# First MLP product in three float32r products of 12-bit parts, in place of a seven-product float32 scheme

## The chip, the cores and the metric

The kernel runs on one core of a Trainium2 chip, in one launch. The metric is the device time of the program in microseconds, as the median of several runs. Three runs of the kernel before gave 356.90, 357.06 and 355.76 us: a median of 356.9.

## What is computed

The first part is a state-space layer (Mamba2) over 4 batches, 8 heads, 768 tokens, head dimension 32 and state dimension 16. The second is a two-layer MLP with a hard-swish between its products. Cut to what matters:

```
for each chunk of tokens:                  # x, a, B, C are inputs; float32
    cum   = cumsum(log(clip(a)))
    M     = (C B^T) * exp(cum_i - cum_j), causal
    y     = M x + (C state) * exp(cum_i)
    state = exp(cum_end) * state + sum_j exp(cum_end - cum_j) B_j x_j
X = y reordered to (3072 tokens, 256)
h = X @ w_in                               # 256 x 2048
g = h * clip(h + 3, 0, 6) / 6
out = g @ w_out                            # 2048 x 256
```

The weights arrive as 8-byte floats (their raw words are read) and are decoded to float32 on the chip.

## The kernel before, in words

**Blocks.** The 768 tokens are cut into 6 blocks of 128. Block `k` of all four batches is 512 columns of MLP work. The outer loop `for k in range(NC)` (L993) runs the MLP of block `k` and, woven in between, the attention part of block `c = k + 1` and loads and decays of block `ahead = k + 2`. The order of every engine's queue is the order in which the program text issues the instructions (the pools run under a manual schedule), and each engine works its queue in that order. SP issues nearly all DMAs, in the same way.

**Decoding of weights.** `decode(i)` (L187) turns one of eight pieces of 8-byte words into float32: pieces 0 to 3 are `w_in` (512 of the 2048 columns each, both halves of the contraction), pieces 4 to 7 are `w_out`. Each piece is five steps: an ACT copy (L198), three VectorE operations on integers (L215, L217, L201), two ACT activations (L221, L223) with a VectorE operation (L205), and two VectorE operations that finish (L228, L236). Pieces 0 and 1 are made before block 0's product, the others are woven into it.

**Block 0.** `mlp_in` (L613) makes a column tile `f` of `h` (128 of the 2048 hidden columns by 512 tokens) with two float32 matmuls of 128x512. ACT's `ramp` (L694) takes Relu(h/6 + 1/2) into `gT` and VectorE's `times_ramp` (L699) caps it at 1 and multiplies it by `h`. Four PSUM banks (f0 to f3) rotate. Then `first_out` (L703) makes the output with plain products, and VectorE makes sums of weights (`weight_sums`, L729; `in_weight_sums`, L632). The attention of block 1 is placed between its parts; `results(c)` runs `mix` (the last attention matmuls), `keep` (four ACT copies of y from PSUM to `yT`, L608) and `sum_y` (four VectorE sums of y halves, L655). Two tiles later `lead(c, 0)` begins the product of block 1.

**Blocks 1 to 5, first product.** Hidden columns are taken in pairs of tiles (`s` of 8), and a 2x2 block scheme with seven products of 128x256 in place of eight computes both (`lead`, `early`, `middle`, `last`; every matmul is L658). It uses sums of `w_in` made once and sums of `yT` made per block. In each pair, ACT copies a partial product to a second bank (L673) and one to SBUF (L680), VectorE copies one (L674) and adds two (L686, L687); then come two `ramp` and two `times_ramp`.

**Blocks 1 to 5, second product.** `wide_units` (L827, matmuls L836; the last block `out_units`, L760, matmuls L772) makes the output with a seven-product scheme, in 14 steps of 8 float32 matmuls; the loop over these steps carries `scores`, `multiply`, `decay_ends`, `results` of the next block. At step 12 the next block's `lead` is issued. GpSimd makes the sums of `gT` for it (`g_sums`, L758), the masks (`conceal`, L158) and some small products (L396, L403).

Of the kernel before, what the change touches and what calls it, by code (L numbers as in the profile page):

```python
# [8 lines left out]
FP32 = mybir.dt.float32  # L9
U32 = mybir.dt.uint32  # L10
# [10 lines left out]
def kernel(  # L21
# [34 lines left out]
    NQ = NH // 2  # L56
    HU = NH // 2
# [57 lines left out]
    def load_x(c):  # L115
        sl = slice(c * P, (c + 1) * P)
        xts[c] = loads.tile([P, NB * NH, D], FP32, name="xt")
        nc.sync.dma_start(out=xts[c], in_=x[:, :, sl, :].rearrange("b h s d -> s (b h) d"))

    w_in = const.tile([P, NK, DF], FP32, name="w_in")  # L120
    w_sum = const.tile([P, NF // 2, P], FP32, name="w_sum")
# [50 lines left out]
    nc.vector.memset(half, 0.5)  # L172
    bias_hi = const.tile([P, 1], FP32, name="bias_hi")
# [12 lines left out]

    def decode(i):  # L187
# [7 lines left out]
        s = att.tile([P, n], U16, name="ws")  # L195
        e = att.tile([P, n], U16, name="we")
# [33 lines left out]
        if i < NP:  # L230
            dst = w_in[:, :, i * FP * P:(i + 1) * FP * P]
            m, e = (t.rearrange("p (k f) -> p k f", k=NK) for t in (m, e))
        else:
            dst = w_out[:, (i - NP) * FP:(i - NP + 1) * FP, :]
            m, e = (t.rearrange("p (k f) -> p k f", k=FP) for t in (m, e))
# [8 lines left out]
    picks = const.tile([P, G * N], BF16, name="picks")  # L244
# [77 lines left out]

    yTs, states, mids, bTs, bss, tmps = {}, {}, {}, {}, {}, {}
# [67 lines left out]
    def ends(c, b):  # L391

        if b == 0:
            bss[c] = att.tile([P, G, N], FP32, name="bs")
        hs = slice(b * NH, b * NH + NH)
        nc.gpsimd.tensor_tensor(  # L396
            out=bss[c][:, hs], in0=Bs[c][:, hs],
            in1=Ls[c][:, b, :, HT - 1:HT].to_broadcast([P, NH, N]), op=ALU.mult)
# [174 lines left out]
    def renew(c):  # L573

        states[c] = att.tile([P, NB, 2 * D], FP32, name="state")
        later = att.tile([P, NB, 2 * D], FP32, name="later", bufs=1)
        nc.vector.tensor_tensor(
            out=later, in0=mids[c], in1=etos[c][:, :, P - 1:P].to_broadcast([P, NB, 2 * D]),
            op=ALU.mult)
        new_state(states[c], adds[c], later)  # L580
# [22 lines left out]
    def keep(c):  # L603

        yTs[c] = att.tile([P, NK, NB, P], FP32, name="yT")
        for a, u in ((0, 0), (0, 1), (1, 0), (1, 1)) if c else ((0, 0), (1, 0), (0, 1), (1, 1)):
            y, dst = ys[c][a, u], yTs[c][:, u, :, HALF[a]]
            nc.scalar.copy(out=dst, in_=y)  # L608
# [4 lines left out]
    def mlp_in(k, f):  # L613
        h = ps.tile([P, NK, 2 * P], FP32, name="h", tag=f"f{f % 4}")
        for j in range(NK):
            nc.tensor.matmul(  # L616
                out=h.rearrange("p r i -> p (r i)"), lhsT=w_in[:, j, f * P:(f + 1) * P],
                rhs=yTs[k][:, j].rearrange("p b i -> p (b i)"),
# [10 lines left out]
    wi = w_in.rearrange("p k (j e c) -> p k e j c", e=2, c=P)  # L629
    in_sums, y_sums, evens, odds, parts_of = {}, {}, {}, {}, {}  # L630

    def in_weight_sums():  # L632
        for h in range(2):
            js = slice(h * NJ // 2, (h + 1) * NJ // 2)
            a11, a12, a21, a22 = (wi[:, k, e, js] for e in range(2) for k in range(2))
            s1, s2 = (att.tile([P, NJ // 2, P], FP32, name="w_sum", tag=t) for t in ("ws", "we"))
            s4 = w_sum[:, js]
            for o, p_, q_, op in ((s1, a21, a22, ALU.add), (s2, s1, a11, ALU.subtract),
                                  (s4, a12, s2, ALU.subtract), (a21, a11, a21, ALU.subtract)):
                nc.vector.tensor_tensor(out=o, in0=p_, in1=q_, op=op)  # L640
            for n, t in ((1, s1), (2, s2), (3, a21), (4, s4)):
                in_sums.setdefault(n, []).extend(t[:, i] for i in range(NJ // 2))
            yield

    def y_half(k, j, r):
        return yTs[k][:, j, 2 * r:2 * r + 2].rearrange("p b i -> p (b i)")

    def sum_y(k):
        ts = att.tile([P, 3, 2 * P], FP32, name="ts", bufs=1)
        t1, t2, t4 = (ts[:, i] for i in range(3))  # L650
        t3 = y_half(k, 0, 1)
        y_sums[k] = {1: t1, 2: t2, 3: t3, 4: t4}
        for o, p_, q_ in ((t1, t3, y_half(k, 0, 0)), (t3, y_half(k, 1, 1), t3),
                          (t2, y_half(k, 1, 1), t1), (t4, y_half(k, 1, 0), t2)):
            nc.vector.tensor_tensor(out=o, in0=p_, in1=q_, op=ALU.subtract)  # L655

    def half_product(bank, r, lhsT, rhs, start=False):
        nc.tensor.matmul(  # L658
            out=bank[:, r], lhsT=lhsT, rhs=rhs, start=start, stop=True, skip_group_check=True)

    def lead(k, s):

        (pool, tag), (pool_e, tag_e) = (
            ((ps, "f0"), (ps, "f2")), ((ps, "f1"), (ps, "f3")),
            ((ps_y, "y0"), (ps_y, "y1")))[s % 3]
        odds[k, s] = odd = pool.tile([P, 2, 2 * P], FP32, name="odd", tag=tag)
        evens[k, s] = even = pool_e.tile([P, 2, 2 * P], FP32, name="even", tag=tag_e)
        parts_of[k, s] = up = ffn.tile([P, 2, 2 * P], FP32, name="up", bufs=2)  # L670
        half_product(odd, 1, wi[:, 0, 0, s], y_half(k, 0, 0), start=True)
        half_product(odd, 0, in_sums[3][s], y_sums[k][3])
        nc.scalar.copy(out=even, in_=odd[:, 1:2].to_broadcast([P, 2, 2 * P]))  # L673
        nc.vector.tensor_copy(out=up[:, 1], in_=odd[:, 0])  # L674

    def early(k, s):
        even = evens[k, s]
        half_product(even, 0, wi[:, 1, 0, s], y_half(k, 1, 0))
        half_product(even, 1, in_sums[2][s], y_sums[k][2])
        nc.scalar.copy(out=parts_of[k, s][:, 0], in_=even[:, 1])  # L680

    def middle(k, s):
        even, odd, up = evens[k, s], odds[k, s], parts_of[k, s]
        half_product(odd, 0, wi[:, 1, 1, s], y_sums[k][4])
        half_product(even, 1, in_sums[1][s], y_sums[k][1])
        nc.vector.tensor_tensor(out=odd[:, 0], in0=odd[:, 0], in1=up[:, 0], op=ALU.add)  # L686
        nc.vector.tensor_tensor(out=odd[:, 1], in0=even[:, 1], in1=up[:, 1], op=ALU.add)  # L687

    def last(k, s):
        half_product(evens[k, s], 1, in_sums[4][s], y_half(k, 1, 1))  # L690
# [12 lines left out]
    def first_out(b, i, c):  # L703
# [6 lines left out]
        for f in range(i * FP, (i + 1) * FP):  # L710
            if b == NB - 1 and f == NF - 2:
                lead(c, 0)
            nc.tensor.matmul(  # L713
                out=o[:, b % 2], lhsT=gTs[0][:, f, b * P:(b + 1) * P], rhs=w_out[:, f],
                start=(f == 0 and b % 2 == 0), stop=True, skip_group_check=True)
        if i == NP - 1 and b % 2:
            ob = ffn.tile([P, 2, DM], FP32, name="ob", bufs=2)
# [11 lines left out]
    def weight_sums():  # L729


        t3 = const.tile([P, NJ, P], FP32, name="t3")
# [27 lines left out]
    def out_units(k):  # L760
# [15 lines left out]
        for t in range(2):  # L776
# [9 lines left out]
            if t == 0:  # L786
                unit(oa, 0, quarter(0, 0, 0), w4[:, 0, 0], rest)
                unit(oa, 3, quarter(0, 0, 1), w4[:, 0, 0], rest)
                x1 = ffn.tile([P, 2, P], FP32, name="x1")
# [6 lines left out]
            res = ffn.tile([P, 5, P], FP32, name="res", bufs=2)  # L796
# [7 lines left out]
            u = ffn.tile([P, 2, P], FP32, name="u", bufs=2)  # L804
# [108 lines left out]
    def results(c, parts=range(2)):  # L913
        mix(c, parts)
        keep(c)
        sum_y(c)
# [4 lines left out]

    def load(c):
        load_bc(c)
        load_x(c)
# [60 lines left out]
    load(1)  # L985


    weave = {}
# [4 lines left out]
    for k in range(NC):  # L993
        gTs[k] = ffn.tile([P, NF, TB], FP32, name="gT")
        c, ahead = k + 1, k + 2
        if k == 0:
            for f in range(NF):
                mlp_in(k, f)
                for i in weave.get(f, []):
                    weights(i, 1)  # L1000
                if f in (6, 8):
                    diff_exp(c, f // 2 - 3)
            load(ahead)
# [3 lines left out]
            sums, sums_in = weight_sums(), in_weight_sums()  # L1007
            for i in range(NP):
                for b in range(NB):
                    first_out(b, i, c)  # L1010
                    if (i, b) == (0, 0):
                        weights(NP + 3, 1)
                        weights(NP + 2, 1)
                        weights(NP + 3, 3)
                        rows(ahead)
                    elif (i, b) == (1, 0):
                        next(sums_in)
                        next(sums_in)
# [16 lines left out]
                    elif (i, b) == (3, 1):  # L1035
                        results(c)
                        next(sums)
                        decay_ends(ahead, 3)
                    elif (i, b) == (3, 3):
# [3 lines left out]
        for s in range(NJ):  # L1043
            early(k, s)
            if s == 0:
                if ahead < NC:
                    load(ahead)
                if c < NC:
                    carry(c)
            if s < NJ - 1:  # L1050
                lead(k, s + 1)
            if s:
                last(k, s - 1)
                ramp(k, 2 * s - 2, evens[k, s - 1])
            middle(k, s)
            if s:
                times_ramp(k, 2 * s - 2, evens[k, s - 1])
            ramp(k, 2 * s + 1, odds[k, s])
            times_ramp(k, 2 * s + 1, odds[k, s])
            if s in (1, 3) and ahead < NC:  # L1060
                conceal(ahead, s // 2)
            if s in (3, 5) and c < TURN:
                turn(c, s // 4)
            if s in (2, 4, 6):
                g_sums(k, s - 2)
        for i, _ in enumerate((wide_units if c < NC else out_units)(k)):
            if i == 0:
                s = NJ - 1
                last(k, s)
                ramp(k, 2 * s, evens[k, s])  # L1070
                times_ramp(k, 2 * s, evens[k, s])
                g_sums(k, s - 1)
                if k == 1:
                    next(sums)
            if c < NC:
# [11 lines left out]
                if i == (7 if c == TURN else 6):  # L1087
                    results(c, (1,) if c == TURN else range(2))
                    if ahead < NC:
                        from_start(ahead)  # L1090
# [4 lines left out]
                if i == 12:  # L1095
                    lead(c, 0)

# [29 lines left out]
```

## Time and profile before

| what | value |
|---|---|
| median of three runs | 356.9 us |
| span of the profiled execution, first to last instruction | 353.6 us |
| TensorE busy | 343.7 us (97%) |
| VectorE busy | 227.4 us (64%) |
| ACT busy | 178.7 us (51%) |
| GpSimd busy | 138.0 us (39%) |
| first product of block 0 (h, L616), in the chain | 22.83 to 50.49 us |
| first product of block 2, with the steps of block 1's output it is mixed with | 137.5 to 163.3 us |
| granted TensorE clock, mean | 1.000 |

The profile lists, for one execution, every instruction with its start and length on its engine. Of that execution the span alone is given; the 3.3 us between it and the median of the runs lie outside the first and last instruction. "PE" is TensorE's matmuls, "PEld" its weight loads, "DVE" VectorE, "ACT" ScalarE, "POOL" GpSimd, "SP" the engine that issues DMAs. In a group's row the first number after the bar is the union of its busy time and the second the mean length of one instruction in ns; matmuls overlap, so the distance between their starts is their pace. A time-line row is start, length, engine, line and operation. The chain of work that ended last is followed back from the last instruction, at each step to what released it.

### The profile page before, as it was taken

To read this page: it belongs to the slowest core of one execution; us is meant where nothing else is said; L and a number is where in the kernel's file an instruction comes from. 1 tells how busy PE (TensorE), PEld (TensorE's weight loads), DVE (VectorE), ACT (ScalarE), POOL (GpSimd) and SP (SyncE) were. 2 spreads that over 40 slices of the span, in tenths; PEclk is the share of its full clock that TensorE was granted. 3 is DMA by queue.
4 is the path that set the end of the run, shared out by engine and by line. 5 is a ranking of instruction groups with operands and counts; after the bars stand their busy time and mean duration, and the time that the engine had idled before them with its cause. 6 is when DMAs were issued, how large, how long until landed. Compare 5 with 4: busy or idle time off the path is not lost.

```text
span 353.6 us, 8557 instructions
## 1 busy us (share of the span) xinstructions
PE 343.7 (97%) x3488; PEld 281.9 (80%) x3488; DVE 227.4 (64%) x426; ACT 178.7 (51%) x394; POOL 138.0 (39%) x139
## 2 busy tenths in 40 slices
PE   6699999999999999999999999999999999999996
PEld 2454458888887888888888888888888888888996
DVE  6689999975797437786437787436687322688111
ACT  4768887258764741665641575551575011466100
POOL 3300000362498621099612099710078600068700
PEclk9999999999999999999999999999999999999999
DMA  8999969502925052256034256001200001200000
GB/s 168 178 335 162 272 157 122 128 2 78 164 55 66 4 125 51 35 70 81 2 72 97 36 67 91 4 4 18 34 9 1 4 3 20 34 8 2 0 32 30
DMA packets 91607, 24.92 MB, mean 70 GB/s; under 512 B 84208, under 2 KB 87952, under 8 KB 91056
## 3 DMA queue, kind: packets, MB, share of 16 engines
q1 hardware_dynamic: 87184, 23.06, 35.7%
q10 hardware_dynamic: 4384, 1.31, 1.7%
q8 instruction: 27, 0.44, 0.5%
q14 instruction: 12, 0.10, 0.1%
HBM read 21.07 MB, written 3.29 MB: 69 GB/s over the span
## 4 chain that ended last, share of the span: by engine, by line
PE 91%; DVE 3%; DMA 3%; ACT 1%; SPq 1%; issue 1%; DVEq 0%; ACTq 0%
PE even L658 18%; PE odd L658 13%; PE wb L836 12%; PE wc L836 8%; PE o L713 8%; PE h L616 8%; PE wa L836 8%; PE oa L772 4%; PE ob L772 4%; PE y L594 3%; PE y L500 2%; PE cb L527 2%; DMA raw<-in_moe_w_in_dram 2%; PE y L539 1%; DMA pairs<-in_C_dram 1%; SPq L100 1%
## 5 line engine op out<-in xcount | busy, mean ns | idle before, releaser
L758 POOL TENSOR_TENSOR s<-gT 128x512 f32<-128x512 f32 x20 | 26.3, 1317 | 86.0 <-DVE gT L699 86.0
L658 PE MATMUL even<-ts,w_sum 128*128 128x256 f32 x160 | 48.2, 383 | 0.0
L694 ACT ACTIVATE gT<-odd,half 128x512 f32<-128x512 f32 x40 | 27.5, 688 | 34.9 <-DVE odd L687 34.9
L658 PE MATMUL odd<-yT,w_in 128*128 128x256 f32 x160 | 41.1, 379 | 0.0
L673 ACT COPY even<-odd 128x512 f32<-128x512 f32 x40 | 23.0, 576 | 27.7 <-PE odd L658 25.5
L658 PEld LDWEIGHTS even<-ts,w_sum 128*128 128x128 f32 x160 | 29.9, 190 | 5.3 <-ACT up L680 1.5
L699 DVE SCALAR_TENSOR_TENSOR gT<-gT,odd 128x512 f32<-128x512 f32 x40 | 27.5, 688 | 9.9 <-ACT gT L694 9.9
L658 PEld LDWEIGHTS odd<-yT,w_in 128*128 128x128 f32 x160 | 30.4, 190 | 4.1
L385 ACT ACTIVATE L<-L,cum_n 128x64 f32<-128x64 f32 x128 | 31.5, 340 | 0.0
L836 PE MATMUL wb<-s,w_out 128*128 128x256 f32 x128 | 30.7, 382 | 0.0
L694 ACT ACTIVATE gT<-even,half 128x512 f32<-128x512 f32 x40 | 27.8, 695 | 4.4 <-PE even L658 4.4
L699 DVE SCALAR_TENSOR_TENSOR gT<-gT,even 128x512 f32<-128x512 f32 x40 | 27.2, 679 | 4.4 <-ACT gT L694 4.4
L713 PE MATMUL o<-w_out,gT 128*128 128x256 f32 x128 | 28.7, 381 | 0.0
L616 PE MATMUL h<-yT,w_in 128*128 128x512 f32 x64 | 27.7, 594 | 0.0
L674 DVE COPY up<-odd 128x256 f32<-128x256 f32 x40 | 16.9, 423 | 15.8 <-ACT even L673 15.1
L713 PEld LDWEIGHTS o<-w_out,gT 128*128 128x128 f32 x128 | 24.1, 190 | 3.7 <-issue 0.5
L403 POOL TENSOR_TENSOR tmp<-state,eto 128x256 f32<-128x256 f32 x5 | 3.4, 684 | 60.4 <-DMA eto<-cum_e 51.1
L836 PEld LDWEIGHTS wb<-s,w_out 128*128 128x128 f32 x128 | 24.0, 190 | 3.4
L758 POOL TENSOR_TENSOR s<-s,gT 128x512 f32<-128x512 f32 x20 | 25.5, 1273 | 1.6
L758 POOL TENSOR_TENSOR gT<-gT 128x512 f32<-128x512 f32 x20 | 25.4, 1272 | 0.0
L758 POOL TENSOR_TENSOR s<-gT,s 128x512 f32<-128x512 f32 x20 | 25.4, 1270 | 0.0
L658 PE MATMUL even<-yT,w_sum 128*128 128x256 f32 x80 | 24.4, 387 | 0.2
(150 smaller groups left out, 657.9 us busy)
## 6 DMA issues: line engine op xcount, KB each, us to landing
raw<-in_moe_w_out_dram SPq DMA_DIRECT2D x4, 1024.0 KB
L<-cum_d SPq DMA_DIRECT2D x8, 512.0 KB
xt<-in_x_dram SPq DMA_DIRECT2D x6, 512.0 KB
raw<-in_moe_w_in_dram SPq DMA_DIRECT2D x3, 1024.0 KB
out_dram<-back SPq DMA_DIRECT2D x128, 16.0 KB
eto<-cum_e SPq DMA_DIRECT2D x20, 64.0 KB
B<-in_B_dram SPq DMA_DIRECT2D x5, 256.0 KB
raw<-in_moe_w_in_dram ACTq DMA_DIRECT2D x1, 1024.0 KB
```

The source lines that it names most:

```text
L385: nc.scalar.activation(Ls[c][:, b, h], Ls[c][:, b, h], AF.Exp, bias=cum_n[:, c, g:g + 1])
L594: nc.tensor.matmul(out=ys[c][a, u][d0:d0 + D, b], lhsT=xt[rows, b * NH + h], rhs=Ls[c][rows, b, h], start=(b == 0 and a >= min(c, 1)), sto ...
L616: nc.tensor.matmul(out=h.rearrange("p r i -> p (r i)"), lhsT=w_in[:, j, f * P:(f + 1) * P], rhs=yTs[k][:, j].rearrange("p b i -> p (b i)") ...
L658: nc.tensor.matmul(out=bank[:, r], lhsT=lhsT, rhs=rhs, start=start, stop=True, skip_group_check=True)
L673: nc.scalar.copy(out=even, in_=odd[:, 1:2].to_broadcast([P, 2, 2 * P]))
L674: nc.vector.tensor_copy(out=up[:, 1], in_=odd[:, 0])
L694: nc.scalar.activation(gTs[k][:, f], h.rearrange("p r i -> p (r i)"), AF.Relu, bias=half, scale=1.0 / 6.0)
L699: nc.vector.scalar_tensor_tensor(out=g, in0=g, scalar=1.0, in1=h.rearrange("p r i -> p (r i)"), op0=ALU.min, op1=ALU.mult)
L713: nc.tensor.matmul(out=o[:, b % 2], lhsT=gTs[0][:, f, b * P:(b + 1) * P], rhs=w_out[:, f], start=(f == 0 and b % 2 == 0), stop=True, skip_ ...
L758: nc.gpsimd.tensor_tensor(out=o, in0=p_, in1=q_, op=op)
L772: nc.tensor.matmul(out=bank[:, slot], lhsT=lhs[:, j], rhs=rhs[:, j], start=(clear and j == 0), stop=True, skip_group_check=True)
L836: nc.tensor.matmul(out=bank[:, slot], lhsT=lhs[:, j], rhs=rhs[:, j], start=(clear and j == 0), stop=True, skip_group_check=True)
```

## The change

The first product of blocks 1 to 5 is no longer the seven-product scheme. With Z = 2^-12, each weight and each y is cut into a high part and a low part scaled by 1/Z, and a third tile "gap" = high - low holds their difference. Then h = (1 + Z) high.high + (Z + Z^2) low.low - Z gap.gap, so three products give it. Their tiles have the type float32r. In `lead(k, f)` the gap product of a column tile is made and scaled in PSUM by -Z/(1 + Z), by ACT for even tiles and VectorE for odd ones; `follow(k, f)` adds the other two products in the same bank. Six banks rotate, and lead runs two tiles ahead.

The parts of y are made in `split_y` behind `keep` (ACT and VectorE), in place of `sum_y`; the parts of the weights once, in `split_w`, in block 0, by ACT and GpSimd. Block 0 keeps its float32 product, from decoded tiles (`first_in`) that are given up later. `w_in`, `w_sum` and `in_weight_sums` go. To make room, several tiles share buffers; `xt` and `bs` have one buffer, and the load of x is issued behind `results`.

```diff
+    def split_w(i):
+        high, low, gap = (
+            [t[:, j, i * FP * P:(i + 1) * FP * P] for j in range(NK)]
+            for t in (w_high, w_low, w_gap))
+        for j, w in enumerate(first_in[i]):
+            nc.scalar.mul(high[j], w, CUT)
+            nc.gpsimd.tensor_tensor(out=low[j], in0=w, in1=high[j], op=ALU.subtract)
+        yield
+        for j in range(NK):
+            nc.scalar.mul(low[j], low[j], 1.0 / Z)
+            nc.gpsimd.tensor_tensor(out=gap[j], in0=high[j], in1=low[j], op=ALU.subtract)
+        yield
+
+    def split_y(k):
+        for j, y in enumerate(yTs[k]):
+            copy_y(k, 1, j)
+            high, low, gap = (y_tile(n, FP32R) for n in ("high", "low", "gap"))
+            nc.scalar.mul(high, y, CUT)
+            nc.vector.tensor_tensor(out=low, in0=y, in1=high, op=ALU.subtract)
+            nc.vector.scalar_tensor_tensor(
+                out=gap, in0=low, scalar=-1.0 / Z, in1=high, op0=ALU.mult, op1=ALU.add)
...
+    def in_product(h, w, y, f, start=False):
+        for j in range(NK):
+            nc.tensor.matmul(
+                out=h, lhsT=w[:, j, f * P:(f + 1) * P], rhs=y[j],
+                start=(start and j == 0), stop=True, skip_group_check=True)
+
+    def lead(k, f):
...
+        hs[k, f] = h = pool.tile([P, TB], FP32, name="h3", tag=tag)
+        in_product(h, w_gap, gaps[k], f, start=True)
+        if f % 2:
+            nc.vector.tensor_scalar(
+                out=h, in0=h, scalar1=-Z / UP, scalar2=None, op0=ALU.mult)
+        else:
+            nc.scalar.mul(h, h, -Z / UP)
+
+    def follow(k, f):
+        h = hs.pop((k, f))
+        in_product(h, w_high, highs[k], f)
+        in_product(h, w_low, lows[k], f)
+        g = gTs[k][:, f]
+        nc.scalar.activation(g, h, AF.Relu, bias=half_up, scale=UP * UP / 6.0)
+        nc.vector.scalar_tensor_tensor(
+            out=g, in0=g, scalar=UP, in1=h, op0=ALU.min, op1=ALU.mult)
...
     def results(c, parts=range(2)):
         mix(c, parts)
         keep(c)
-        sum_y(c)
+        split_y(c)
...
                 mlp_in(k, f)
                 for i in weave.get(f, []):
                     weights(i, 1)
+                if f % 4 == 1:
+                    next(splits[f // 4])
+                if f and f % 4 == 0:
+                    next(splits[f // 4 - 1])
...
                         weights(NP + 3, 3)
+                        next(splits[NP - 1])
                         rows(ahead)
-                    elif (i, b) == (1, 0):
-                        next(sums_in)
-                        next(sums_in)
...
-        for s in range(NJ):
-            early(k, s)
+        for f in range(NF):
...
+            if f + 2 < NF:
+                lead(k, f + 2)
+            follow(k, f)
...
                 if i == 12:
                     lead(c, 0)
+                    lead(c, 1)
```

## Prediction

> **What bounds the kernel now.** I read the page's busy times first, then the chain of work that ended last, then the groups of TensorE by shape, then the busy times of a stretch, and last the time line where VectorE and GpSimd run side by side. Page of before:
>
> ```profile
> span 353.6 us, 8557 instructions
> ...
> PE 343.7 (97%) x3488; PEld 281.9 (80%) x3488; DVE 227.4 (64%) x426; ACT 178.7 (51%) x394; POOL 138.0 (39%) x139
> ...
> PEclk9999999999999999999999999999999999999999
> ...
> PE 91%; DVE 3%; DMA 3%; ACT 1%; SPq 1%; issue 1%; DVEq 0%; ACTq 0%
> ```
>
> TensorE ends the kernel: 91% of the chain is its own work, at a full granted clock. So a change is worth the TensorE time it removes, less the time it makes TensorE wait. The groups by shape:
>
> ```profile
> L658 PE MATMUL even<-ts,w_sum 128*128 128x256 f32 x160 | 48.2, 383 | 0.0
> L658 PE MATMUL odd<-yT,w_in 128*128 128x256 f32 x160 | 41.1, 379 | 0.0
> ...
> L658 PE MATMUL even<-yT,w_sum 128*128 128x256 f32 x80 | 24.4, 387 | 0.2
> L658 PE MATMUL even<-yT,w_in 128*128 128x256 f32 x80 | 24.2, 384 | 0.0
> L658 PE MATMUL odd<-ts,w_in 128*128 128x256 f32 x80 | 23.8, 379 | 0.0
> ...
> L348 PE MATMUL d<-less,split 128*128 128x512 bf16 x8 | 2.4, 382 | 0.9 <-DVE split L280 0.9
> ```
>
> The first product of blocks 1 to 5 (L658) is 560 records: 5 blocks x 8 pairs x 7 products, two records for each float32 product. A mean of 380 ns is a latency. The pace is in the chain in time order, where "137.49 0.86 PE odd L658 x4" gives 0.216 us a record. 560 x 0.216 = 121.0 us.
>
> **What is removed and added on TensorE.** The new form has 5 blocks x 16 column tiles x 3 products x 2 halves of the contraction = 480 matmuls of 128x512. Whether each is one pass no float32r row of this trace tells. The nearest rows: a bf16 matmul of 128x512 has the same latency as a float32 record of 128x256 (382 and 383 ns), so a float32 record streams its 256 columns twice and the bf16 one its 512 once; the pair of L348 that starts at 7.47 lasts 0.60 us, which less the 0.38 of one is a pace of 0.22. One pass is therefore 0.216 us, and nothing here streams 512 columns faster. Two passes would be 0.432 (the h rows of L616: 27.66 us for 64 records of 128x512). I take one pass, by the bf16 row: 480 x 0.216 = 103.7 us, and 121.0 - 103.7 = **17.3 us saved**. The weight load of each record should hide: the loads of L658 last 190 ns, and the 128x128 rows of L772 keep a pace of 0.112 us (16 records in 1.80 us), load included.
>
> [...]
>
> **ACT and VectorE inside the product.** For each pair of column tiles TensorE needs 2 x 6 x 0.216 = 2.59 us. ACT has two Relus (L694, 0.69) and one scaling in PSUM (as L673, 128x512, 0.58): 1.96 us. VectorE has two products with the ramp (L699, 0.69) and one scaling (as L447, 0.68): 2.06 us. Both fit, and six banks leave the scaling some 2 us between lead and follow. Block 1 also carries the transposes of C (L441, L447: 2.1 us of VectorE), which already cost it about 1.2 us of gaps; 0.3 us more in all. The sums of y and of w_in (L655, L640) go; VectorE had room for them, so that is worth nothing.
>
> **The start of block 1.** Before, ACT starts the four copies to yT at 81.02 and TensorE starts lead at 82.81. Now lead needs both gap tiles: four copies (0.28 apart) and two multiplications (0.53 apart, as L389 of 0.64) end near 83.2, and the last two VectorE operations (0.69 each) near 85. TensorE stands before the second gap matmul at 83.2: it waits about **2 us**. In blocks 2 to 5 six wide steps of 1.73 us lie between the mix and lead and hide it; without them it would be the same 2 us each.
>
> **Block 0.** The parts of the weights are made while TensorE runs h and o from 22.8 to 77. They are 16 ACT multiplications (0.64) and 16 GpSimd subtractions of 128x512 (L758 shape, 1.27). GpSimd idles there, but VectorE does not, and the last weights are decoded only 1 to 1.6 us ahead of TensorE (w_in's third piece ends at 35.1, used at 36.7; the fourth at 42.6, used at 43.6; w_out's first at 49.6, used at 50.5):
>
> ```profile
> 22.80:64.90 42.10, 42.10 (x134) 25.06 (x133) 39.63 (x59) 32.94 (x39) 0.00 (x0) 1.00 1.05 190
> ```
>
> The columns are length, then PE, PEld, DVE, ACT and POOL busy: VectorE 39.6 of 42.1 us, ACT 32.9, GpSimd nothing. ACT's 16 x 0.57 = 9.1 us more bring it to 42: alone that delays TensorE by about 1 us, since gaps of 4 us in its queue fill first. The dearer part is that VectorE and GpSimd stop each other. Time line where both work on SBUF:
>
> ```profile
> 112.43 1.27 POOL L758 TENSOR_TENSOR s<-gT,s 128x512 f32<-128x512 f32 x1
> ...
> 113.20 1.57 DVE L740 TENSOR_TENSOR w_out<-w_out 128x1024 f32<-128x1024 f32 x1
> 113.66 2.25 POOL L758 TENSOR_TENSOR s<-gT 128x512 f32<-128x512 f32 x1
> 115.98 1.28 POOL L758 TENSOR_TENSOR s<-s,gT 128x512 f32<-128x512 f32 x1
> ```
>
> And earlier, a GpSimd copy beside casts of one source:
>
> ```profile
> 4.82 1.01 POOL L258 COPY picks<-pick 128x512 bf16<-128x512 bf16 x1 [2.13 <-DVE parity L260]
> ...
> 5.46 0.52 DVE L276 CAST split<-pre 32x256 bf16<-32x256 f32 x1
> ...
> 6.46 0.28 DVE L278 CAST pre<-pre 32x256 bf16<-32x256 f32 x1
> ```
>
> L740 takes 1.22 us alone and 1.57 here: it began 0.35 us late, so the GpSimd subtraction held it from 112.43 to 113.55, that is 1.13 us. Then GpSimd's next one waited about 1 us for VectorE (2.25 for 1.27). The cast with one source did so too (0.52 against 0.28). L699, which reads PSUM, keeps its 0.69 beside GpSimd (112.60). All decode operations of VectorE are of the two kinds that wait, about 4.4 us for each of the weight pieces; the 16 L699 of block 0, 0.6 apart, are not. So VectorE in that stretch is about 29.4 us that needs the port, 9.6 us that does not, and 2.5 us idle. Fourteen of the 16 subtractions fall before the last piece of w_in and w_out's first two pieces are done: 14 x 1.13 = 15.8 us of port. *Upper end*: none lies beside port-free time; 15.8 less 1.4 us of lead = 14.4. *Lower end*: all 12.1 us free of the port cover it, 15.8 - 12.1 - 1.4 = 2.3; with no lock only ACT's 1 us stays. A subtraction meets a port operation in 29.4/39 = 0.75 of the cases: 11.9, less 1.4 of lead, less about 1.5 of the idle time = **9 us** that TensorE waits in block 0, before the third and fourth w_in pieces and the first two w_out pieces. I take that, as both orders of waiting stand in the rows above.
>
> [...]
>
> **Moved transfers.** x of the next block is loaded behind the mix, with one buffer; SP issues it ahead of the decay rows, which wait for the same mix. It is read some 25 us later. Nothing on the path; if late, into_state waits for it.
>
> **Sum.** 353.6 - 17.3 + 0.3 + 2.0 + 9.0 = 347.6 us of span. The median of the runs is 356.9, 3.3 us above the span of the profiled execution, which I keep: **350.9 us**.
>
> **Rivals.**
> - *The port costs little* (0 to 5 us): GpSimd's work falls beside L699 and VectorE's waits. For it: 12.1 us of port-free time. Against: back-to-back alternation in the rows above. With 3 us: 344.9.
> - *The port is not covered at all*: 14.4 us, and 356.3, no change that can be told.
> - *The new matmuls are not one cheap pass* (the change doesn't do what it says, and the slower side): place, the 480 records; price, 480 times what each takes over 0.216 us. It decides from (17.3 - 11.3)/480 = 0.0125 us more, a pace of 0.2285. A weight load that does not hide behind 512 columns, at 0.25 us, gives 350.9 + 16.3 = 367; two passes give 350.9 + 103.7 = 455. For it: no float32r row in the trace. Against: loads of the same 4-byte size hide at 0.112 us.
>
> **How the numbers follow.** Forecast (block 0 loses 5 to 12 us) 0.56; little cost 0.20; uncovered 0.09; slower matmuls 0.15. A difference of 0.5% (1.8 us) is about what can be told from no change. Faster takes the first two, 0.76; same 0.09; slower 0.15. The range holds all but the slower matmuls: from a block-0 loss of 1 us (342.9, rounded to 342.5) to 14.4 plus some late lead (358).
>
> **What would show it.** The new records at a pace of 0.216 and 103.7 us in all; in block 0, TensorE gaps before h's column tiles 8 and 12 and the first o, VectorE decode rows longer by up to 1.1 us where GpSimd runs; GpSimd subtractions of 2 us and more; a gap of 2 us before the second new matmul. Wrong if the records' pace is over 0.2285, if block 0 ends within 2 us of its old length, or if the out phases of blocks 1 to 4 grow.

## The result, and the profile after

The changed kernel is slower: a median of 360.3 us against 356.3, a ratio of 1.0116 with a 95% interval of 1.0077 to 1.0154, so the loss of 1.2% is small but clear of the spread. The forecast was 350.9 us, and the range ended at 358.0. The profiled execution has a span of 356.9 us (before: 353.6) and took 358.7 us; the four runs have spans of 356.9 to 359.8.

The page of the changed kernel:

```profile
span 356.9 us, 8261 instructions
...
PE 337.6 (95%) x3408; PEld 266.9 (75%) x3408; DVE 223.0 (62%) x341; ACT 183.1 (51%) x380; POOL 165.1 (46%) x155
...
PEclk9999999999999999999999999999999999999999
...
PE 77%; DVE 14%; ACT 3%; DMA 3%; issue 1%; SPq 1%; DVEq 0%
```

TensorE's busy time fell by only 6 us, and the chain that ended last is now 77% TensorE and 14% VectorE where it was 91% and 3%: TensorE waits for VectorE somewhere. The stretch in which the weights are decoded shows where. Its columns are length, then PE, PEld, DVE, ACT and POOL busy, the granted clock and the DMA share:

```profile
22.80:64.90 42.10, 35.76 (x94) 17.24 (x95) 40.60 (x46) 34.00 (x48) 21.81 (x14) 1.00 0.73 161
```

In the same 42.1 us TensorE did 94 records where it did 134, VectorE is as full as before but did 46 operations instead of 59, and GpSimd now works 21.8 us. Inside it, TensorE's time line (start, length, and in brackets the idle time before, with what ended it):

```profile
37.01 1.13 PE L641 MATMUL h<-yT,w 128*128 128x512 f32 x2 [0.34 <-DVE w L247]
38.69 2.84 PE L641 MATMUL h<-yT,w 128*128 128x512 f32 x6 [0.55 <-DVE w L247]
42.71 3.70 PE L641 MATMUL h<-yT,w 128*128 128x512 f32 x8 [1.18 <-DVE gT L720]
47.41 1.12 PE L641 MATMUL h<-yT,w 128*128 128x512 f32 x2 [1.00 <-DVE w L247]
```

and VectorE and GpSimd beside it, each from its own time line:

```profile
35.31 3.33 DVE L247 SCALAR_TENSOR_TENSOR w<-wm,wse 128x512 f32<-128x512 f32 x2
...
45.63 3.41 DVE L247 SCALAR_TENSOR_TENSOR w<-wm,wse 128x512 f32<-128x512 f32 x2
```

```profile
34.75 3.34 POOL L667 TENSOR_TENSOR w_gap<-w_high,w_low 128x512 fp32r<-128x512 f32 x2 [3.89 <-ACT w_low L666]
...
45.54 2.95 POOL L667 TENSOR_TENSOR w_gap<-w_high,w_low 128x512 fp32r<-128x512 f32 x2 [4.36 <-ACT w_low L666]
```

The two halves of a decoded piece (L247) take 3.3 us together, where a two-input operation of the same size takes 0.69 (L676, 92.44), while two GpSimd subtractions take 3.3 us, where one took 1.27 before (L758, 112.43): they take turns. TensorE's h waits for `w` of just those rows. That is the stall which the prediction described: it named h's column tiles 8 and 12 and the first o, and 37.01 and 47.41 are tiles 8 and 12. Two waits of 1.18 us, one of them in the rows above (42.71), stand at tiles it had not named: there TensorE waits for `gT` (L720), an operation that keeps its length (a mean of 0.68 us, as L699 had in block 0 before) but stands in VectorE's queue behind the slow ones. Before, the stretch had none of these waits. In TensorE's time line the first transposes, which stand behind h and the first output matmuls, come 9.8 us later; first the row of before, then the row after:

```profile
65.87 0.60 PE L422 MATMUL t_ps<-ident,B 128*128 128x128 f32 x4
```

```profile
75.69 0.60 PE L443 MATMUL t_ps<-ident,B 128*128 128x128 f32 x4
```

Behind block 0 TensorE waits again, for the two gap tiles of y. TensorE's rows, and VectorE's first operation on y:

```profile
94.01 0.47 PE L684 MATMUL h<-gap,w_gap 128*128 128x512 f32 x1 [1.20 <-DVE gap L677]
95.24 0.97 PE L684 MATMUL h<-gap,w_gap 128*128 128x512 f32 x3 [0.77 <-DVE gap L677]
```

```profile
92.44 0.69 DVE L676 TENSOR_TENSOR low<-yT,high 128x512 fp32r<-128x512 f32 x1 [2.31 <-ACT high L675]
```

The new product, by shape:

```profile
L684 PE MATMUL h<-gap,w_gap 128*128 128x512 f32 x160 | 51.7, 408 | 2.0 <-DVE gap L677 2.0
L684 PE MATMUL h<-high,w_high 128*128 128x512 f32 x160 | 50.7, 398 | 0.3 <-DVE h L697 0.3
L684 PE MATMUL h<-low,w_low 128*128 128x512 f32 x160 | 50.3, 395 | 0.0
```

A mean of 395 to 408 ns is some 16 to 25 ns more than the 379 to 383 of the rows it was compared with. The pace is in the chain in time order, where most of block 2's product is one line:

```profile
150.09 21.50 PE h L684 x92
```

21.50 us for 92 records is **0.2337 us a record**, not 0.216, and 480 of them are 112.2 us. Nothing in that line waits. So the change saved 121.0 - 112.2 = 8.8 us and not 17.3.

| term | forecast, us | measured, us | read from |
|---|---|---|---|
| new records against old ones | -17.3 | -8.8 | 480 x 0.2337 against 560 x 0.216 |
| block 0 waits | +9.0 | +9.8 | first output transposes at 75.69, before at 65.87 |
| start of block 1 | +2.0 | +2.4 | second gap matmul at 95.24; 92.86 if it stood as far behind the transposes as the second record of lead did before (82.81 - 65.87, and one record of 0.23) |
| all else | +0.3 | -0.1 | the difference to +3.3 of span |

### The profile page after: what moved, and what is told of

Read it like the earlier page. It is cut to its first block, busy times and chain, and to the rows that moved or that the text cites. A ratio compares the mean times of both kernels' runs of the same rounds, so it can differ in the third digit from the quotient of the medians.

```text
span 356.9 us, 8261 instructions
## 1 busy us (share of the span) xinstructions
PE 337.6 (95%) x3408; PEld 266.9 (75%) x3408; DVE 223.0 (62%) x341; ACT 183.1 (51%) x380; POOL 165.1 (46%) x155
## 4 chain that ended last, share of the span: by engine, by line
PE 77%; DVE 14%; ACT 3%; DMA 3%; issue 1%; SPq 1%; DVEq 0%
PE h L684 31%; PE wb L861 12%; PE wc L861 8%; PE wa L861 8%; PE o L735 4%; PE oa L794 4%; PE ob L794 4%; DVE gT L720 3%; PE y L615 2%; PE y L521 2%; DVE w L247 2%; PE cb L548 2%; DMA raw<-in_moe_w_in_dram 2%; ACT L L406 2%; DVE wse L225 2%
## 5 line engine op out<-in xcount | busy, mean ns | idle before, releaser
L708 DVE SCALAR_TENSOR_TENSOR gT<-gT,h 128x512 f32<-128x512 f32 x80 | 55.0, 688 | 33.5 <-ACT gT L707 30.5
L707 ACT ACTIVATE gT<-h,half_up 128x512 f32<-128x512 f32 x80 | 55.2, 690 | 36.2 <-PE h L684 36.2
L684 PE MATMUL h<-gap,w_gap 128*128 128x512 f32 x160 | 51.7, 408 | 2.0 <-DVE gap L677 2.0
L684 PE MATMUL h<-high,w_high 128*128 128x512 f32 x160 | 50.7, 398 | 0.3 <-DVE h L697 0.3
L684 PE MATMUL h<-low,w_low 128*128 128x512 f32 x160 | 50.3, 395 | 0.0
L684 PEld LDWEIGHTS h<-gap,w_gap 128*128 128x128 f32 x160 | 29.9, 188 | 9.2 <-ACT high L675 1.6
L684 PEld LDWEIGHTS h<-high,w_high 128*128 128x128 f32 x160 | 29.6, 188 | 8.6 <-DVE h L697 1.8
L684 PEld LDWEIGHTS h<-low,w_low 128*128 128x128 f32 x160 | 30.1, 188 | 7.3
L641 PE MATMUL h<-yT,w 128*128 128x512 f32 x64 | 29.3, 603 | 4.8 <-DVE w L247 2.4
L406 ACT ACTIVATE L<-L,cum_n 128x64 f32<-128x64 f32 x128 | 31.4, 337 | 0.0
L589 DVE TENSOR_TENSOR L<-L,cb 128x512 f32<-128x512 f32 x24 | 15.3, 681 | 22.8 <-PE cb L548 19.7
L697 DVE TENSOR_SCALAR h<-h 128x512 f32<-128x512 f32 x40 | 27.7, 692 | 1.2 <-PE h L684 1.2
L641 PEld LDWEIGHTS h<-yT,w 128*128 128x128 f32 x64 | 11.6, 189 | 21.8 <-issue 10.4
L162 POOL TENSOR_SCALAR_AFFINE_SELECT L<-L 64x1024 f32<-64x1024 f32 (+1 forms) x16 | 18.6, 1166 | 17.3 <-DMA L<-cum_d 17.0
```

Of the source, the lines that this page charges most:

```text
L162: nc.gpsimd.affine_select(out=t[rows], in_=t[rows], pattern=pattern, compare_op=ALU.is_ge, fill=-1e5, base=base, channel_multiplier=-1)
L406: nc.scalar.activation(Ls[c][:, b, h], Ls[c][:, b, h], AF.Exp, bias=cum_n[:, c, g:g + 1])
L641: nc.tensor.matmul(out=h.rearrange("p r i -> p (r i)"), lhsT=first_in[f // FP][j][:, f % FP * P:(f % FP + 1) * P], rhs=yTs[k][j], start=(j ...
L684: nc.tensor.matmul(out=h, lhsT=w[:, j, f * P:(f + 1) * P], rhs=y[j], start=(start and j == 0), stop=True, skip_group_check=True)
L697: nc.vector.tensor_scalar(out=h, in0=h, scalar1=-Z / UP, scalar2=None, op0=ALU.mult)
L707: nc.scalar.activation(g, h, AF.Relu, bias=half_up, scale=UP * UP / 6.0)
```

## The experiments

Two questions were open: what in block 0 costs the 9.8 us (GpSimd beside VectorE, or ACT's longer queue), and why a float32r record takes 0.234 us. Each kernel is the changed one with the edit shown, cut to what matters; the last three go further and move or replace the parts.

**Block 0 without the subtractions.**

```diff
-            nc.gpsimd.tensor_tensor(out=low[j], in0=w, in1=high[j], op=ALU.subtract)
...
-            nc.scalar.mul(low[j], low[j], 1.0 / Z)
-            nc.gpsimd.tensor_tensor(out=gap[j], in0=high[j], in1=low[j], op=ALU.subtract)
+            nc.scalar.mul(low[j], high[j], 1.0 / Z)
...
-        in_product(h, w_gap, gaps[k], f, start=True)
+        in_product(h, w_low, gaps[k], f, start=True)
```

> The changed kernel without its 16 GpSimd subtractions; ACT makes the low part from the high part instead (so ACT keeps its 16 multiplications) and the gap product reads the low weights. What is left out: the weights' low and gap parts hold other numbers. Theory 1 (GpSimd and VectorE stop each other at SBUF): block 0 gets back about 9 us, the first float32r matmul starts near 85 us of the span instead of 95.2, and the time is near 351. Theory 2 (ACT's queue is what delays block 0): the first float32r matmul stays near 95 and the time near 360.

Measured: 351.4 us, a ratio to before of 0.985 (0.982 to 0.988). The decoding stretch, with the columns of above:

```profile
22.80:64.90 42.10, 41.28 (x127) 24.00 (x128) 37.75 (x58) 40.08 (x55) 0.00 (x0) 1.00 0.88 186
```

and, in TensorE's time line, the first of the transposes of the output:

```profile
66.84 0.60 PE L443 MATMUL t_ps<-ident,B 128*128 128x128 f32 x4
```

ACT is at 40.1 of 42.1 us, and TensorE loses 1.0 us (66.84 against 65.87 before), as was reckoned for ACT alone. The other 8.9 us of the changed kernel's delay (75.69 against 66.84) go with the subtractions.

**Block 0 without ACT's multiplications.**

```diff
-            nc.scalar.mul(high[j], w, CUT)
-            nc.gpsimd.tensor_tensor(out=low[j], in0=w, in1=high[j], op=ALU.subtract)
+            nc.gpsimd.tensor_tensor(out=low[j], in0=w, in1=first_in[i][1 - j], op=ALU.subtract)
...
-            nc.scalar.mul(low[j], low[j], 1.0 / Z)
-            nc.gpsimd.tensor_tensor(out=gap[j], in0=high[j], in1=low[j], op=ALU.subtract)
+            nc.gpsimd.tensor_tensor(out=gap[j], in0=first_in[i][j], in1=low[j], op=ALU.subtract)
...
-        in_product(h, w_high, highs[k], f)
+        in_product(h, w_low, highs[k], f)
```

> The changed kernel without the 16 ACT multiplications of the weights; the 16 GpSimd subtractions stay, with decoded weights as operands, and the high product reads the low weights. What is left out: the weights' parts hold other numbers. Theory 1 (shared port): the first float32r matmul stays at 93 to 96 us. Theory 2 (ACT's queue): it goes to about 85 us.

Measured: 360.1 us in a single run, and the second gap matmul at 96.34 (95.24 in the changed kernel). TensorE's time says little here: its granted clock was 0.61 from 22.8 to 32 us, and ahead of h 16 matmuls of y (L521) took 1.04 us of the chain against 0.61; h began 2.1 us later (24.74 against 22.67), and the mean clock of the stretch was 0.88:

```profile
22.80:64.90 42.10, 38.16 (x161) 18.40 (x147) 40.73 (x49) 28.05 (x36) 20.41 (x15) 0.88 0.67 154
```

VectorE's time can be compared. With ACT lightened to 28 us it is still full with 49 operations (40.7 of 42.1 us). From the end of the third piece of `w_in` to the end of the fourth it needs 9.6 us (41.07 to 50.65), against 10.4 in the changed kernel (38.64 to 49.04) and 7.5 before (35.07 to 42.56). So the subtractions cause most of the loss on VectorE there, with or without ACT's multiplications.

**The pace: half the columns a record.** Each matmul was cut into two of 256 columns, each with its own weight load.

```diff
+            for r in range(2):
+                cols = slice(r * TB // 2, (r + 1) * TB // 2)
...
-                out=h, lhsT=w[:, j, f * P:(f + 1) * P], rhs=y[j],
-                start=(start and j == 0), stop=True, skip_group_check=True)
+                    out=h[:, cols], lhsT=w[:, j, f * P:(f + 1) * P], rhs=y[j][:, cols],
+                    start=(start and j == 0 and r == 0), stop=True, skip_group_check=True)
```

> The changed kernel with every float32r matmul cut into two of 256 columns, each with its own weight load: 960 records. Theory A (a fixed cost of about 18 ns for each record on top of the stream, such as a weight load that is not fully hidden): a pace of 0.125 us, 120 us in all, 8 us more than the 112 of the changed kernel. Theory B (float32r columns stream 8% slower): a pace of 0.117 us and 112 us in all, the time unchanged.

Measured: 363.1 us in a single run. A block's product in the chain:

```profile
151.66 21.72 PE h L686 x184
```

0.118 us a record with twice the weight loads, so the extra goes with the columns, not with the records: about 0.45 ns a column and 2 ns a record, worked out from 0.2337 us at 512 columns and 0.118 at 256. The weight load, which the prediction named as the way in which the pace could be worse, is not it. (Of the 4.4 us of span over the changed kernel, 1.4 lie before the second gap matmul, which came at 96.65, and 2.2 in block 4's output, where 8 matmuls of wb took 3.61 us of the chain (296.44) against 1.92 in the changed kernel (293.91).)

**The pace: a quarter.** The same edit with four of 128 columns.

> The changed kernel with each float32r matmul cut into four of 128 columns, 1920 records. From 0.118 us at 256 columns and 0.234 at 512, a straight line (0.453 ns a column and 2 ns a record) gives 0.060 us and 115 us in all, unless the weight load shows: 128x128 float32 records keep 0.112 us with two passes, so a load that takes that long would give 0.112 us and 215 us in all, the time over 450.

Measured: 461.1 us, and per block

```profile
171.69 41.04 PE h L686 x368
```

0.1115 us a record, where the straight line of the two wider runs gives 0.060, an estimate. So the records of 128 columns have a floor. The weight loads follow each other at the same 0.111 us (8 of 0.19 us each take 0.97 us, 200.00), so the load is the likely floor, an estimate too: no run shows it apart from the matmul. (The 0.112 us of the 128x128 float32 rows is no second reading of it: half of the 0.216 us of 256 columns is 0.108 by itself.) At 512 columns (0.234) the floor is far away.

**The pace: bf16.** All parts in bf16, the rest as it was.

```diff
-        const.tile([P, NK, DF], FP32R, name=n) for n in ("w_high", "w_low", "w_gap"))
+        const.tile([P, NK, DF], BF16, name=n) for n in ("w_high", "w_low", "w_gap"))
...
-            high, low, gap = (y_tile(n, FP32R) for n in ("high", "low", "gap"))
+            high, low, gap = (y_tile(n, FP32).bitcast(BF16)[:, :TB] for n in ("high", "low", "gap"))
```

> The changed kernel with all parts of the product in bf16 instead of float32r (what is left out: four bits of each part). If the slow pace belongs to 4-byte parts, the records go at 0.216 us, 103.7 us in all, and each of blocks 2 to 5 is 1.7 us shorter; if it belongs to 512 columns with a new weight each time or to the PSUM accesses of ACT and VectorE beside it, they stay at 0.234.

Measured: 349.6 us in a single run, with

```profile
147.07 19.97 PE h L684 x92
```

0.2171 us a record. The same program, banks and neighbours on ACT and VectorE give the pace that was forecast; so it is the 4-byte parts that are slow, and not the PSUM accesses beside them.

**The pace: one column of y.** The matmul reads the first column of its part 512 times.

```diff
-                out=h, lhsT=w[:, j, f * P:(f + 1) * P], rhs=y[j],
+                out=h, lhsT=w[:, j, f * P:(f + 1) * P], rhs=y[j][:, 0:1].to_broadcast([P, TB]),
```

> The changed kernel with each float32r matmul of blocks 1 to 5 reading one column of its part of y 512 times (what is left out: all other columns of y). If the pace of 0.234 us comes from reading 512 different 4-byte columns out of SBUF (banks, traffic of other engines), it falls towards 0.217 us and the blocks 2 to 5 are 1.5 us shorter each. If it belongs to how TensorE streams this type, it stays at 0.234.

Measured: 355.6 us in a single run, with block 2's product at

```profile
152.80 20.07 PE h L684 x92
```

0.2182 us. The float32r type itself streams at nearly the bf16 pace when one place is read. (Block 0 was slower here: 16 matmuls of y (L521, 21.59) took 1.05 us of the chain against 0.61 in the changed kernel, and the mean granted clock of the run was 0.98.)

**The pace: one value in all columns.** To tell the reading from the values, the parts were made from y's first column and stored 512 times.

```diff
-            nc.scalar.mul(high, y, CUT)
-            nc.vector.tensor_tensor(out=low, in0=y, in1=high, op=ALU.subtract)
+            y0 = y[:, 0:1].to_broadcast([P, TB])
+            nc.scalar.mul(high, y0, CUT)
+            nc.vector.tensor_tensor(out=low, in0=y0, in1=high, op=ALU.subtract)
```

> The changed kernel with parts of y that hold one value in all 512 columns (the parts are made from y's first column; what is left out: the other columns of y), read as 512 separate columns. If the faster pace of the one-column run (0.218 us) came from reading one place of SBUF, the records go back to 0.234 us here; if it came from values that do not change, they stay at 0.217 to 0.218.

Measured: 360.3 us in a single run, and

```profile
151.73 21.50 PE h L685 x92
```

0.2337 us again. Type, values and neighbours are those of the run before, and only the places read differ: it is the reading of 512 different 4-byte places, whatever they hold.

**The pace: bf16 parts 4 bytes apart.**

```diff
-            high, low, gap = (y_tile(n, FP32R) for n in ("high", "low", "gap"))
+            high, low, gap = (y_tile(n, FP32).bitcast(BF16)[:, 0:2 * TB:2] for n in ("high", "low", "gap"))
```

> The bf16 run with the parts of y stored 4 bytes apart (every other bf16 of the same tiles), so that TensorE walks the same 2048 bytes for 512 columns as it does for float32r. If the slow pace comes from walking 4 bytes a column in SBUF, the records go at 0.234 us instead of 0.217; if it comes from the 4-byte type, they stay at 0.217.

Measured: 355.0 us in a single run, between the two answers. A few records of each block are missing in this trace; the unbroken part of block 2's product is

```profile
148.55 8.84 PE h L684 x39
```

0.2267 us a record, and the product's two ends (148.55 to 169.40 for 92 records) give 0.2266. Walking 4 bytes a column costs about half of the extra with half of the bytes used (0.2266 less 0.2171, of 0.2337 less 0.2171). That agrees with a limit in the reading of y, and does not tell what the limit is.

**The parts of the weights made after the decoding.** High parts by ACT behind tiles 9 and 13 and the last one, low parts by VectorE once the last piece is decoded, gap parts by GpSimd behind the masks.

```diff
-            nc.gpsimd.tensor_tensor(out=low[j], in0=w, in1=high[j], op=ALU.subtract)
...
+            nc.vector.tensor_tensor(out=low[j], in0=w, in1=high[j], op=ALU.subtract)
...
-                if f % 4 == 1:
-                    next(splits[f // 4])
-                if f and f % 4 == 0:
-                    next(splits[f // 4 - 1])
+                if f in (9, 13):
+                    next(splits[f // 12])
...
+                    elif (i, b) == (1, 0):
+                        for s in splits:
+                            next(s)
```

> The changed kernel with the weights' parts made later: the high parts by ACT behind tiles 9 and 13 of block 0 and behind its last tile, the low parts by VectorE behind the last decoded piece (where the sums of w_in were made before), the gap parts by GpSimd behind the masks and at the start of block 1. Theory 1 (shared port during the decoding): the decoding has its port to itself again, the first output transposes come at 66 to 67 us (75.9 in the changed kernel, 66.0 before), the first float32r matmul near 86, span near 348, time near 351, faster than before by 1.4%. Theory 2 (the parts cost the same wherever they stand): the first float32r matmul stays over 92 us and the time near 359.

Measured: 353.3 us, a ratio of 0.993 (0.989 to 0.996): faster than before, by half of what was expected. The decoding is whole again (transposes at 65.57), but the subtractions still meet VectorE, now where block 1 starts. VectorE's and then GpSimd's time line, and TensorE's:

```profile
80.29 2.18 DVE L766 TENSOR_TENSOR t<-t,w_out 128x1024 f32<-128x1024 f32 x1
...
82.40 1.75 DVE L680 TENSOR_TENSOR low<-yT,high 128x512 fp32r<-128x512 f32 x1
```

```profile
79.14 4.46 POOL L671 TENSOR_TENSOR w_gap<-w_high,w_low 128x512 fp32r<-128x512 f32 x2
```

```profile
85.11 0.77 PE L688 MATMUL h<-gap,w_gap 128*128 128x512 f32 x1 [2.43 <-ACT L L406]
86.53 1.62 PE L688 MATMUL h<-gap,w_gap 128*128 128x512 f32 x3 [0.66 <-DVE gap L681]
```

The `low` of y takes 1.75 us instead of 0.69, the sum of weights ahead of it (L766) 2.18 us instead of 1.34, and TensorE stands for 2.4 and 0.7 us. (The first wait is put down to a decay of ACT that ended at the same moment; `gap` ended at 84.96, 0.15 us ahead of the matmul, which is the distance in the changed kernel too.) Three gap matmuls then take 1.62 us where they took 0.97. The stretches (same columns as above; the eighth number is the granted clock) show why:

```profile
84.00:86.00 2.00, 0.77 (x1) 0.29 (x1) 1.93 (x4) 1.11 (x5) 1.23 (x3) 0.71 1.51 150
86.00:88.00 2.00, 1.47 (x4) 1.21 (x5) 2.00 (x2) 0.58 (x1) 2.00 (x2) 0.50 0.01 1
88.00:90.00 2.00, 2.00 (x6) 1.63 (x5) 1.21 (x2) 0.11 (x1) 2.00 (x2) 0.50 0.03 8
```

The clock was cut to half for nearly 7 us (0.58 still from 90 to 92), and block 1's product took 27.2 us (86.53 to 113.71) against 24.8 in the changed kernel. The run without subtractions lost its clock at the same place (0.64 and 0.50 from 86 to 90 us), after waits of 1.2 and 0.8 us; the changed kernel had the same two waits and kept 1.00 (from 92 to 100 us). So these waits, the longest of them 2.4 us, do not by themselves explain when the clock falls, and no run shows what does.

**The same with eight decay activations put behind the parts of y.**

```diff
                         next(sums)
-                        decay_ends(ahead, 2)
...
+                        decay_ends(ahead, 2)
                         decay_ends(ahead, 3)
```

> The late split with 8 of the 24 decay activations that ACT does ahead of the copies of y in block 0 put behind the parts of y. If the wait before the second gap matmul (2.0 us, 9.0 of the chain in ACT and VectorE) is ACT's queue and not the chain of operations itself, the first float32r matmul comes about 2 us earlier than in the late split; if the eight are paid later in the first scalings, the second block's start does not move.

Measured: 353.1 us in a single run. The second gap matmul comes as long after the first output transposes as in the late split (86.53 less 65.57 is 21.0 us there; 87.35 less 66.48 is 20.9 here). VectorE's time line shows why nothing was won:

```profile
81.20 2.18 DVE L766 TENSOR_TENSOR t<-t,w_out 128x1024 f32<-128x1024 f32 x1
...
83.31 1.75 DVE L680 TENSOR_TENSOR low<-yT,high 128x512 fp32r<-128x512 f32 x1
```

`low` still began only when the sum of weights (L766, 2.18 us), slowed by GpSimd's gap parts, was done: in the chain it follows at once (83.39, behind 81.20 and 2.18). So in these two kernels VectorE's queue ends the wait, not ACT's. In the changed kernel it is otherwise: there VectorE stood idle for 2.31 us before `low` and waited for ACT's high part. What moving the decays would do there was not run. The clock stayed at 1.00 at this place, with waits of 2.4 and 0.9 us, and block 1's product took 24.8 us.

**Cross products in bf16, no gap.** h = high.high in float32r, plus high.low and low.high with bf16 parts; the parts of the weights late, by ACT and VectorE alone.

```diff
-        in_product(h, w_gap, gaps[k], f, start=True)
-        if f % 2:
-            nc.vector.tensor_scalar(
-                out=h, in0=h, scalar1=-Z / UP, scalar2=None, op0=ALU.mult)
-        else:
-            nc.scalar.mul(h, h, -Z / UP)
+        in_product(h, w_high, highs[k], f, start=True)
...
-        in_product(h, w_high, highs[k], f)
-        in_product(h, w_low, lows[k], f)
+        in_product(h, w_near, lows[k], f)
+        in_product(h, w_low, gaps[k], f)
```

> As the late split, but with h = high.high in float32r plus the two cross products high.low and low.high in bf16 (parts of 8 bits there; the product low.low, 2 to the -24 of the whole, is left out). No gap tiles, no scaling in PSUM, no GpSimd. If the pace of 0.234 us belongs to float32r records and 0.217 to bf16 ones, a block is 16 x (2 x 0.234 + 4 x 0.217) = 21.4 us of TensorE against 22.4, the lead no longer waits for two VectorE operations for each half, the span is near 341 and the time near 344. If the pace is set by the PSUM accesses beside it, the float32r records go faster than 0.234 here, as the scaling is gone.

Measured: 342.9 us, a ratio of **0.962** (0.955 to 0.968): faster than before and than the changed kernel. One block's product:

```profile
138.59 20.58 PE h L685 x92
```

0.2237 us a record, as 2 x 0.234 and 4 x 0.217 give (0.2227). With the scaling in PSUM gone the float32r records are no faster (an estimate: six records of 0.2237 us less four of 0.2171 leave 0.237 for each of the two), which again clears ACT and VectorE.

## Why the prediction was wrong

- **The pace of the new records: wrong, and it decided.** The step that failed is "One pass is therefore 0.216 us, and nothing here streams 512 columns faster", and with it "480 x 0.216 = 103.7 us" and "17.3 us saved". The record takes 0.2337 us, far from the 0.432 of two passes but not the 0.216 taken for one: 8.5 us of the 9.3 by which the span missed. The bf16 row was the wrong neighbour in one respect: its columns are 2 bytes wide. The float32 rows of L658 read 4-byte columns too and still keep 0.216 us for a record of 256; why the limit does not show in them no run tells. That bf16 at the same stride loses about half as much (0.2266 us against 0.2171), and one column read 512 times loses nearly nothing (0.2182), puts the cost in the reading of y. It was the one step that decided the sign: the other terms of the sum came out within 0.8 us each.
- **The break-even: right, its reason wrong.** The text put the slower side at a pace over 0.2285 and gave it 0.15, with an unhidden weight load or a second pass as the cause. The pace did pass 0.2285, but twice the loads at 256 columns changed next to nothing (2 x 0.118 against 0.2337 us), and the floor that shows at 128 columns is 0.112 us, far below. The chance was too low for a type that no row of the trace showed.
- **Block 0: right in cause, and in size partly by luck.** It was 9.8 us against 9. Without the subtractions 1.0 us is left, which is what had been reckoned for ACT; the rows in which VectorE and GpSimd take turns show how the rest arises. What the prediction calls the port and the lock is no more than this taking of turns: no run shows what the two engines share. The 9 stood between bounds of 2.3 and 14.4 and rested on a share of 0.75 (the parts of VectorE's time there add up to 41.5 of 42.1 us; with 30.0 in place of 29.4 the share is 0.76). Two of the waits stood at tiles that were not named. Single-source operations wait too: the two bit operations of L223 and L225 have means of 0.70 and 0.90 us against 0.42 and 0.43.
- **The start of block 1: right (2.4 against 2.0).** The rows show the chain that was forecast: ACT's copies and multiplication, then two VectorE operations for each half. ACT starts this chain late because its queue holds decays until then (L406 to 90.48, the first copy to yT at 90.84); the run that moved eight of them says nothing on it, as VectorE's queue ended the wait there.
- **ACT and VectorE inside the product: right.** The line of 92 records has no wait; the scaling fits.
- **What else moved.** In block 5, TensorE stood 1.3 us in the last y matmuls with no releaser in the trace (292.3 us); the other kernels with the new product show 1.3 to 1.7 us there and before shows none. Its cause stays open; shorter gaps elsewhere paid for it. In two of these kernels (256 columns a record, and the decays put later) the 8 matmuls of wb behind it took 3.61 and 3.31 us of the chain where the others took 1.92; the mean granted clocks of these two runs were 0.986 and 0.995.
- **From span to time.** The 3.3 us between the profiled span and the median do not all lie outside the first and last instruction, as was taken: in the changed kernel's profiled execution that part is 1.8 us (358.7 less 356.9), and the rest is the spread between executions.
- **Left open:** what exactly limits the reading of 4-byte columns, why 2-byte values 4 bytes apart lie half way, and why the granted clock fell behind some short waits and not behind others.

## What to carry to other kernels

A price taken from a neighbouring row holds only if the row matches in everything that is read: the type's width was the difference here (0.2337 us against 0.2171), and 8% on 480 instructions turned a gain into a loss. Before a cheap engine is given work, look at what its neighbour does at that moment: two-input and single-source VectorE operations on SBUF and GpSimd operations took turns here, so 16 subtractions on an idle GpSimd cost 9 us beside a full VectorE. And where a product is made of one large term and small corrections, the corrections can go in a cheaper type: with bf16 cross products the third operand, the scaling and GpSimd's subtractions all went, and the time was 342.9 us.

## What the runs showed of the hardware

- A float32r matmul of 128x512 takes 0.2337 us in a stream, 256 columns 0.118 us, against 0.217 us for bf16; reading one column 512 times gives 0.218 us, the same value in 512 places 0.2337 us, bf16 at 4-byte steps 0.2266 us.
- A float32r record of 128 columns with its own weight load takes 0.1115 us, where a straight line through 512 and 256 columns gives 0.060, an estimate; that the load is the floor is an estimate too, which no run shows apart.
- VectorE and GpSimd operations on SBUF took turns: a pair of 128x512 VectorE operations (L247, 35.31) took 3.3 us beside GpSimd subtractions, and one of 128x1024 (L254) 2.18 us beside them (56.03) and 1.23 us where GpSimd stood idle (26.15).
- Behind short TensorE waits the granted clock fell in some kernels and not in others. It was 0.64 and 0.50 from 86 to 90 us after waits of 1.2 and 0.8 us (no subtractions), 0.50 to 0.71 from 84 to 92 us with waits of 2.4 and 0.7 us (late split), and stayed at 1.00 after 1.2 and 0.8 us in the changed kernel and after 2.4 and 0.9 us with the decays later. Block 1's product took 27.2 us in the late split against 24.8 in the changed kernel.
